# Sums of Mish activations made in SBUF for eleven of the twelve quads, with the order of issue made anew

## The chip, the cores and the metric

The kernel runs on one core of one Trainium2 chip. The metric is device time of one execution in microseconds (us); lower is better. Five engines each run their own list of instructions in order: TensorE (PE in the profile), VectorE (DVE), ScalarE (ACT), GpSimd (POOL) and SyncE (SP), which issues most of the DMAs. [...]

## The reference

Two blocks read the same activations `x` (2048 tokens, 640 features, float32), and a sigmoid gate mixes their results.

```python
x = A_x
g = _sigmoid((x * gate_w).sum(-1, keepdims=True))
a = _A_ref(x, A_wqkv, A_wo)          # 32 heads of 20, window of 8 positions, dilation 2
b = _B_ref(x, B_w1, B_b1, B_w2)      # 640 -> 1728, Mish, -> 640
return g * a + (1 - g) * b
```

```python
h = jnp.einsum("bsd,df->bsf", x, w1) + b1
sp = jnp.log1p(jnp.exp(-jnp.abs(h))) + jnp.where(h > 0, h, jnp.zeros_like(h))
act = h * jnp.tanh(sp)
return jnp.einsum("bsf,fd->bsd", act, w2)
```

## The kernel before

**Products.** Every float32 operand of TensorE is split into a high part (ScalarE, L458) and a low part (VectorE or GpSimd, L461), and each product is made of three matmuls (L517 to L519). Many products are arranged in the manner of Strassen and Winograd: blocks of two row groups by two column groups are made with seven products in place of eight, from sums of operands made beforehand.

**Quads.** The first product of block B (`x` by `w1`) is done in twelve quads. `quad(q, P, R)` makes the four blocks of hidden rows `q` and `q + 7` for the token blocks `2P` and `2P + 1`; q runs from 0 to 5 and P over 0 and 1, and a quad's number is q + 7P, so 0 to 5 and 7 to 12. A quad has eight groups of matmuls on TensorE, 54 matmuls in all, in the PSUM banks `one`, `five`, `two_`, `three` and `four`; there are seven banks for all users. Between the groups stand ScalarE copies from bank to bank (L1061). Two results end in the banks `one` and `two_`; the other two need a further addition on VectorE (`closed`, L1011 or L1094), which leaves them in the SBUF tiles `z12` and `z5`. Mish is applied to all four.

**What the second product needs.** The second product (`w2`) again works with sums of the four activations 11, 12, 21, 22 of a quad: t1 = 11 - 12, t3 = 22 - 12, t2 = 22 + t1 and t4 = t2 - 21 (12 and 21 are stored with their sign turned). All seven, 11, 21, 22 and t1 to t4, go to blocks in DRAM (`act...` and `actt...` in the profile), since they are read much later.

**The two ways to make the sums.** In `mish` (L860) every activation is put into the DRAM blocks, the first addend by plain DMA on SyncE's queue (`put`, L853), the further ones by accumulating DMAs issued by GpSimd (`plus`, L856, issue at L857); of the four `plus` of a quad two take their addend from DRAM. An activation's SBUF tile is free as soon as these transfers have read it. In `added` (L1000) the four activations stay in SBUF: m11 and m12 in the two buffers of the ring `hb`, the others in `z12` and `z5` of the ring `z` (four buffers). L1006 and L1008 are its Mish and sign change. The raw 11, 21 and 22 are put to DRAM; then `total` (L1015), on VectorE or GpSimd, adds in place: t1 into m11, t3 into m12, t2 into z5, t4 into z12, and each is put to DRAM. An addition in place waits until the put of the value that it overwrites has landed; t2 waits for t1 and t3, t4 for t2. Both ways have seven puts for a quad. The set `ADDED` names the quads of the second kind: before, quad 11 alone.

**Order.** The program is recorded as some 2,750 tasks, and a table `ISSUE` gives by their numbers the order for each engine, written out in full; `TAKEN` gives for each buffer ring which engine's task takes the next buffer. `Plan.run` walks through these lists, assigns buffers and banks by its own estimates (`LAG`, `ADDING`, the `size` of a DMA), and makes GpSimd's additions wait for the start of certain VectorE instructions (`follow`). The estimates don't reach the chip; the order, the buffers and the waits do. Loads and stores share SyncE's one list, `plus` and GpSimd's arithmetic share GpSimd's. Between the quads stand the q, k, v products of attention (`qkv`, two to a head group, 15 matmuls each); VectorE works through the attention (L570 to L617) all the while. `mlp1_rest` (L1101) makes the last 64 hidden rows in a flat tile of the ring `pair` (23 places).

Of the kernel before, what the change touches and what calls it, by code (L numbers as in the profile page):

```python
# [25 lines left out]
ROW = 2 * QF  # L26
# [12 lines left out]
ADDED = set([11])  # L39
# [27 lines left out]
class Task:  # L67
# [8 lines left out]
    "PE": """1 96-110 115 120 125 130 145 135 140 232 290 240 236 244 267 298 294 263 302 376 377 380 381 386 388 425 389 390 426 429 430  # L76
435 464 437-439 487 488 491 492 456 497 499 468 460 500 501 536 544 540 548 619 620 623 624 629 631 632 650 651 633 654 655
660 662 663 681 664 739 740 685 693 743 744 689 749 751-753 770 774 778 782 914 909 893 944 919 929 924 945 948 949 954 956
957 1066 1067 958 1070 1071 1076 1078 1107 1079 1080 1102 1097 1112 1175 1176 1179 1180 1185 1187 1206 1188 1189 1246 1210
1218 1247 1250 1251 1214 1256 1289 1301 1297 1293 1258-1260 1357 1358 1403 1361 1362 1364 1366-1368 1404 1407 1408 1413 1415  # L80
1440 1416 1417 1443 1442 1441 1457 1458 1480 1479 1460 1459 1481 1493 1494 1530 1529 1508 1495 1482 1507 1509 1531 1496 1532
1510 1555 1556 1558 1628 1557 1627 1629 1778 1630 1779-1789 1799 1800 1825 1826 1836 1837 1871-1882 1924-1935 1945 1946 1958
1959 1969 1970 1996-2007 2035-2042 2049 2050 2060 2061 2071 2072 2088-2095 2137-2144 2163 2164 2174 2175 2185 2186 2205-2212
2235-2246 2256 2257 2269 2270 2280 2281 2300-2311 2344-2355 2365 2366 2376 2377 2387 2388 2404-2415 2441-2448 2455 2456
2468-2478 2572 2479 2573 2577 2578 2593 2582 2584 2587 2594 2598 2590 2599 2603 2605 2627 2608 2704 2631 2611 2729 2705 2730
2734 2709 2735 2710 2726 2714 2739 2741 2716 2744 2719 2747 2722 2751""",
    "ACT": """7 4 10 13 16 19 25 31 22 47 28 44 41 35 38 116 56 121 72 50 117 59 126 118 62 111 122 53 119 131 127 128 76 123 136 124 146
137 90 132 147 112 141 78 113 142 160 94 88 114 129 74 148 143 233 291 149 163 234 133 212 134 209 144 241 138 242 228 139
92 184 154 237 166 226 224 230 187 238 243 239 292 245 246 169 299 235 190 293 295 268 264 269 286 252 303-305 300 296 378
# [97 lines left out]
class Plan:  # L187
# [3 lines left out]
    ADDING = 5400  # L191
# [133 lines left out]
def kernel(ctx: ExitStack, tc: tile.TileContext, x, wq, wo, w1, b1, w2, out):  # L325
# [1427 lines left out]
```

## Time and profile before

| | us |
|---|---|
| median of 3 runs | 620.06 (619.36, 620.06 and one of 3496.55) |
| the profiled execution | 620.14 |
| its span | 618.4 |
| DVE busy | 563.1 |
| ACT busy | 390.1 |
| mean granted TensorE clock | 0.996 |

The span reaches from the first to the last instruction that the profiler saw. The 2,669 matmuls are pipelined: a row of the timeline gives 0.39 us for one of 512 columns, but the next starts 0.23 us later, so starts are what is compared. PE busy is the share of the time in which at least one runs. A busy engine need not be the bound; a wait on TensorE is.

By line, the page has 26, 13 and 11 issues of accumulating DMAs at L857 from DRAM blocks, from `hb` and from `z`, and 2 more from `pair`: 52.

### The profile page before, as it was taken

How to read it: one execution, taken by the hardware profiler on the slowest of the kernel's cores; microseconds unless marked ns; L12 is line 12 of the kernel's file. 1: busy time of each engine (PE TensorE's matmuls, PEld its weight loads, DVE VectorE, ACT ScalarE, POOL GpSimd, SP SyncE). 2: the span in 40 equal slices, each digit the busy share in tenths (PEclk: the TensorE clock that was granted, in tenths of full speed). 3: DMA queues.
4: the chain of work that ended last, by engine and by line, in shares of the span. 5: the costliest groups of instructions: out<-in, count | busy, mean ns of one | idle time of the engine just before them, and what ended most of it. 6: DMA issues, size and time to landing. Idle time of an engine off the chain costs nothing.

```text
span 618.4 us, 8933 instructions
## 1 busy us (share of the span) xinstructions
PE 608.9 (98%) x2669; PEld 501.1 (81%) x2669; DVE 563.1 (91%) x519; ACT 390.1 (63%) x878; POOL 348.3 (56%) x327
## 2 busy tenths in 40 slices
PE   9999999999999999899999999999999999999997
PEld 6888888877887888688888888887778888888886
DVE  5489999999998999879999999999999999998872
ACT  6564765667757667683478778476777563495640
POOL 2444655545365863575468658968756594614330
PEclk9999999999999999899999999999999999999999
DMA  9636499799999999999999999999999999996733
GB/s 320 215 108 197 121 260 300 194 284 252 296 236 290 234 258 281 276 242 298 279 305 270 330 303 295 271 300 299 326 355 323 302 346 317 331 363 215 244 104 137
DMA packets 109298, 165.03 MB, mean 267 GB/s; under 512 B 12464, under 2 KB 51120, under 8 KB 109216
## 3 DMA queue, kind: packets, MB, share of 16 engines
q1 hardware_dynamic: 102144, 151.60, 75.1%
q0 software_dynamic: 7104, 12.85, 13.7%
q8 instruction: 21, 0.34, 0.2%
q14 instruction: 29, 0.24, 0.1%
HBM read 95.45 MB, written 66.40 MB: 262 GB/s over the span
## 4 chain that ended last, share of the span: by engine, by line
PE 78%; DMA 7%; DVE 4%; ACT 4%; issue 3%; POOL 2%; SPq 2%; ACTq 0%; POOLq 0%; DVEq 0%
PE bank L517 25%; PE bank L519 25%; PE bank L518 25%; POOL pair L461 2%; SPq L467 2%; DMA raw<-in_w 1%; DMA pair<-actt 1%; DVE pr L570 1%; ACT pair L458 1%; DMA raw<-in_x 1%; PE bank L659 1%; DMA hb<-in_w 1%; DVE pair L461 1%; DMA raw<-in_wq 1%; DMA act<-pair 1%
## 5 line engine op out<-in xcount | busy, mean ns | idle before, releaser
L518 PE MATMUL bank<-pair,pair 128*128 128x512 f32 (+2 forms) x742 | 288.1, 388 | 0.4 <-POOL pair L461 0.3
L517 PE MATMUL bank<-pair,pair 128*128 128x512 f32 (+2 forms) x742 | 287.9, 388 | 0.7 <-ACT hx L669 0.7
L519 PE MATMUL bank<-pair,pair 128*128 128x512 f32 (+2 forms) x742 | 287.5, 387 | 0.0
L461 POOL TENSOR_TENSOR pair<-raw,pair 128x512 fp32r<-128x512 f32 (+3 forms) x84 | 106.4, 1274 | 103.5 <-ACT pair L458 35.8
L517 PEld LDWEIGHTS bank<-pair,pair 128*128 128x128 f32 x742 | 139.5, 188 | 29.5 <-ACT hx L669 1.1
L518 PEld LDWEIGHTS bank<-pair,pair 128*128 128x128 f32 x742 | 139.5, 188 | 29.3 <-POOL pair L461 1.3
L519 PEld LDWEIGHTS bank<-pair,pair 128*128 128x128 f32 x742 | 139.5, 188 | 28.0 <-POOL pair L461 0.4
L461 POOL TENSOR_TENSOR pair<-pair 128x512 fp32r<-128x512 f32 (+2 forms) x78 | 97.8, 1273 | 37.5 <-DVE pair L461 8.8
L458 ACT ACTIVATE pair<-pair 128x512 fp32r<-128x512 f32 (+2 forms) x147 | 83.2, 609 | 40.2 <-DMA pair<-actt 17.7
L570 DVE TENSOR_TENSOR pr<-kvq,side 128x2560 f32<-128x2560 f32 x32 | 90.1, 2815 | 4.3 <-ACT side L576 3.4
L617 DVE TENSOR_REDUCE kvq<-pr 128x320 f32<-128x2560 f32 x32 | 90.1, 2816 | 0.8
L608 DVE TENSOR_TENSOR pr<-kvq,side 128x2560 f32<-128x2560 f32 x32 | 90.2, 2818 | 0.7
L573 DVE TENSOR_REDUCE lg<-pr 128x128 f32<-128x2560 f32 x32 | 90.0, 2812 | 0.4
L458 ACT ACTIVATE pair<-raw 128x512 fp32r<-128x512 f32 (+4 forms) x123 | 73.2, 616 | 22.4 <-POOL raw L914 7.3
L665 ACT ACTIVATE kvq<-bank 128x320 f32<-128x320 f32 x64 | 27.5, 433 | 43.0 <-PE bank L519 42.9
L914 POOL TENSOR_TENSOR raw<-raw,raw 128x256 f32<-128x256 f32 (+2 forms) x34 | 35.1, 1033 | 25.2 <-DVE pair L461 13.1
L461 DVE TENSOR_TENSOR pair<-pair 128x512 fp32r<-128x512 f32 (+2 forms) x69 | 45.7, 697 | 0.6 <-ACT pair L458 0.4
L517 PE MATMUL bank<-kvq,pair 128*128 128x512 f32 x102 | 40.7, 399 | 3.0 <-ACT bank L1061 3.0
L519 PE MATMUL bank<-kvq,pair 128*128 128x512 f32 x102 | 40.5, 397 | 0.0
L518 PE MATMUL bank<-kvq,pair 128*128 128x512 f32 x102 | 40.3, 395 | 0.0
L1061 ACT ACTIVATE bank<-bank 128x512 f32<-128x512 f32 x36 | 20.9, 582 | 28.7 <-PE bank L519 24.0
L461 DVE TENSOR_TENSOR pair<-raw,pair 128x512 fp32r<-128x512 f32 (+4 forms) x39 | 28.1, 734 | 9.1 <-ACT pair L458 9.1
(138 smaller groups left out, 643.6 us busy)
## 6 DMA issues: line engine op xcount, KB each, us to landing
pair<-actt SPq DMA_DIRECT2D x54, 256.0 KB, 4.5
pair<-act SPq DMA_DIRECT2D x38, 256.0 KB, 4.4
raw<-in_wq SPq DMA_DIRECT2D x36, 248.0 KB, 5.2
raw<-in_w SPq DMA_DIRECT2D x34, 256.0 KB, 3.4
raw<-in_x SPq DMA_DIRECT2D x29, 256.0 KB, 5.4
actt<-hb SPq DMA_DIRECT2D x28, 256.0 KB, 5.4
actt<-z SPq DMA_DIRECT2D x24, 256.0 KB, 4.9
act<-z SPq DMA_DIRECT2D x24, 256.0 KB, 4.3
```

The lines of the kernel that those rows point to most:

```text
L458: a = add("ACT", act_ns(n), lambda: A.activation(hi(), raw(), AF.Copy), after, rank=rank, take=take, hold=hold, kind="hi")
L461: return (V if e == "DVE" else G).tensor_tensor(lo(), raw(), hi().bitcast(F32), op=OP.subtract)
L517: nc.tensor.matmul(ps, ah, bh, start=first, stop=False, skip_group_check=more)
L518: nc.tensor.matmul(ps, ah, bl, start=False, stop=False, skip_group_check=more)
L519: nc.tensor.matmul(ps, al, bh, start=False, stop=last, skip_group_check=more)
L570: return V.tensor_tensor(pr, window(kv, s0, 0), qs[:, :, None, :].to_broadcast([128, 2, W, QF]), op=OP.mult)
L573: return V.tensor_reduce(lg_w[:, s0:s0 + 2], pr.rearrange("p s w (h d) -> p s w h d", d=DH), op=OP.add, axis=AX.X)
L608: return V.tensor_tensor(twos, vw, pw[:, :, :, :, None, None].to_broadcast([128, 2, W, HQ, DH // 2, 2]), op=OP.mult)
L617: return step("DVE", 2740, lambda: V.tensor_reduce(q[:, s0:s0 + 2].rearrange("p s (f j) -> p f s j", j=2), by_place, op=OP.add, axis=AX.X) ...
L665: a = add("ACT", 330, lambda: A.activation(kv[:, 7 + s], ps.t[:, QF:3 * QF].rearrange("p (a b) -> p a b", a=2), AF.Copy), [done] + before, ...
L914: return (V if e == "DVE" else G).tensor_tensor(t.t[:, i:i + n], a.t[:, j:j + n], b.t[:, k:k + n], op=op)
L1061: return add("ACT", 590, lambda: A.activation(to.t, of.t, AF.Copy), after, rank=-0.6, take=[to], hold=[of], kind=kind)
```

## The change

`ADDED` now holds the numbers 0 to 11. Number 6 is no quad and 11 was in it, so ten more quads (0 to 5 and 7 to 10) go through `added`; quad 12 still goes through `mish`. That takes out 40 of the 52 accumulating DMAs and puts 40 additions at L1015 in: in all 44 of them, 36 on GpSimd (4 before) and 8 on VectorE (none before). The number of puts on SyncE's queue is the same, and so is all work of TensorE. Where an addition or a low part may go to VectorE or GpSimd, the new table has some of them changed over; VectorE has 524 rows for 518. ScalarE has 876 rows for 880: activation tables are loaded 21 times for 25, going by the rows at L595, L869 and L1006.

The five tables of `ISSUE` and the strings of `TAKEN` are new throughout. On TensorE the new order differs from the old by changes of place over a few tasks; from task 1778 on it is the same. Estimates of the plan are new as well (`LAG` of SP, `ADDING`, the sizes of five kinds of DMA), which act on the chip only through buffers, banks and waits.

```diff
@@ -36,7 +36,7 @@
-ADDED = set([11])
+ADDED = set([0,1,2,3,4,5,6,7,8,9,10,11])
@@ -73,122 +73,122 @@
 ISSUE = {
-    "PE": """1 96-110 115 120 125 130 145 135 140 232 290 240 236 244 267 298 294 263 302 376 377 380 381 386 388 425 389 390 426 429 430
...
+    "PE": """1 96-110 115 120 125 135 145 130 140 244 232 290 240 236 294 302 263 267 298 376 377 380 381 383 385 425 386 387 426 429 430
...
-    LAG = {"PE": 220, "ACT": 220, "DVE": 200, "POOL": 150, "SP": 2850}
-    ADDING = 5400
+    LAG = {"PE": 220, "ACT": 220, "DVE": 200, "POOL": 150, "SP": 2550}
+    ADDING = 3100
...
-                    after, rank=1.0, hold=hold, size=81920, late=late) for g in range(4)]
+                    after, rank=1.0, hold=hold, size=110592 if late == 0 else 44000, late=late) for g in range(4)]
...
-                            w, rank=-1.0, size=(b - a) * (hi - lo) * ROW * 4) for a, b in ((0, 112), (112, 127))]
+                            w, rank=-1.0, size=(b - a) * (hi - lo) * ROW * (6 if a == 0 else 15)) for a, b in ((0, 112), (112, 127))]
...
-        return dma(lambda: blk[key][rows], src, after, rank=0.5, hold=hold, size=(rows.stop - rows.start) * 2048)
+        return dma(lambda: blk[key][rows], src, after, rank=0.5, hold=hold, size=262144 if rows.stop - rows.start > 64 else 209715)
...
-        d = dma(tall, lambda: h_d[tb], d, hold=[b], size=131072)
+        d = dma(tall, lambda: h_d[tb], d, hold=[b], size=209715)
```

In the quoted list of TensorE, 376 to 390 are the parts of quad 0 (before 376, 377, 380, 381, 386, 388, 389, 390; now 376, 377, 380, 381, 383, 385, 386, 387) and 425 and what follows those of quad 1: the two quads follow one another with no other product between them, before and now.

The two functions of quads that the prediction speaks of are `added`, whose core is this (the same before and after):

```python
        m11, m12 = h_buf(), h_buf()
        a11 = active(q, lambda: one.t, m11, [p2], False, [m11], [one])
        s11 = stored("11", m11, a11)
        a12 = active(q, lambda: two_.t, m12, [p4], True, [m12], [two_])
        ...
        t1 = total(m11, m12, s11 + [a12])
        ...
        t3 = total(m12, z5, [a22, t1])
        t2 = total(z5, m11, s22 + [t1, t3])
        t4 = total(z12, z5, s21 + [t2])
```

and `plus`, which it replaces. Two places show what moved. The first is GpSimd's list in the first half of the quads with P = 1, before. `actt_P_kc_n` and `act_P_kc_n` are DRAM blocks of the activations, `hb` and `z` the SBUF tiles of a quad's activations, `pair` the split operands of TensorE, `raw` tiles that loads arrive in.

```order
L857 DMA actt_1_0_148<-actt_1_0_134 128x512
L857 DMA actt_1_1_135<-hb_2477 128x512
L857 DMA actt_1_0_162<-z_2303 128x512
L461 TENSOR_TENSOR pair_2509<-raw_2193,pair_2509 128x512
L461 TENSOR_TENSOR pair_2506<-raw_2402,pair_2506 128x512
L461 TENSOR_TENSOR pair_2546<-raw_2422,pair_2546 128x496
L461 TENSOR_TENSOR pair_2563<-raw_2431,pair_2563 128x496
L857 DMA actt_1_1_149<-actt_1_1_135 128x512
L461 TENSOR_TENSOR pair_2582<-raw_2535,pair_2582 128x512
L461 TENSOR_TENSOR pair_2569<-raw_2321,pair_2569 128x496
```

Now GpSimd's list has there, for quads 7 and 8:

```order
L1015 TENSOR_TENSOR hb_2252<-hb_2252,hb_2312 128x512
L461 TENSOR_TENSOR pair_2298<-raw_2056,pair_2298 128x512
L1015 TENSOR_TENSOR hb_2312<-hb_2312,z_2225 128x512
L1015 TENSOR_TENSOR z_2225<-z_2225,hb_2252 128x512
L1015 TENSOR_TENSOR z_2314<-z_2314,z_2225 128x512
L461 TENSOR_TENSOR pair_2358<-raw_2267,pair_2358 128x496
L461 TENSOR_TENSOR pair_2377<-raw_2271,pair_2377 128x512
L1015 TENSOR_TENSOR hb_2481<-hb_2481,z_2416 128x512
L461 TENSOR_TENSOR pair_2363<-raw_2175,pair_2363 128x512
L461 TENSOR_TENSOR pair_2511<-raw_2425,pair_2511 128x512
L1015 TENSOR_TENSOR z_2416<-z_2416,hb_2392 128x512
```

The issues of accumulating DMAs are gone, and additions stand between the low parts in their place; a low part now stands behind an addition that may wait for a put.

The second place is ScalarE's list ahead of the first copy of quad 9 from bank to bank, which TensorE's next group waits for. Before:

```order
L458 ACTIVATE pair_2546<-raw_2422 128x496
L872 ACTIVATE z_2453<-z_2453 128x512
L665 ACTIVATE kvq_220<-bank_66 128x320
L458 ACTIVATE pair_2563<-raw_2431 128x496
L667 ACTIVATE kvq_220<-bank_66 128x160
L458 ACTIVATE pair_2569<-raw_2321 128x496
L1061 ACTIVATE bank_68<-bank_63 128x512
```

Now, with the same copy (the source is `bank_63` again) in the third row, and the second copy of the quad in the tenth:

```order
L458 ACTIVATE pair_2553<-raw_2478 128x496
L458 ACTIVATE pair_2558<-raw_2470 128x496
L1061 ACTIVATE bank_69<-bank_63 128x512
L665 ACTIVATE kvq_220<-bank_67 128x320
L667 ACTIVATE kvq_220<-bank_67 128x160
L458 ACTIVATE pair_2571<-raw_2447 128x496
L458 ACTIVATE pair_2581<-raw_2514 128x512
L458 ACTIVATE pair_2584<-raw_2474 128x496
L665 ACTIVATE kvq_220<-bank_65 128x320
L1061 ACTIVATE bank_66<-bank_69 128x512
L458 ACTIVATE pair_2598<-raw_2365 128x512
```

Before, `pair_2546` takes the place that the flat tile of `mlp1_rest` for token block 0 (`pair_2249`) had held, 15 rows behind that tile's last ScalarE instruction; now the tile that follows this flat tile in its place is `pair_2598`, 27 rows behind it and behind both copies.

More of the change, by code (lines that the diff above doesn't have):

```diff
@@ L80 @@
[L80 to L83, printed above, removed]
@@ new lines @@
+2468-2479 2572 2573 2577 2578 2593 2582 2584 2587 2590 2594 2598 2599 2603 2605 2627 2729 2704 2608 2631 2611 2730 2705 2709
+2734 2710 2735 2714 2726 2739 2716 2741 2719 2744 2722 2747 2751""",
+    "ACT": """7 4 19 10 13 16 41 25 47 22 44 31 35 28 38 116 117 59 118 111 72 62 112 56 50 121 126 119 76 53 136 131 122 132 123 74 113
[10 rows of a table added]
+1098-1101 1009 1003 1177 1103 1104 1012 1018 1006 1113 1181 1027 1105 1114 1106 1110 1187 1021 1183 1127 1178 1030 1015 823
+1192 1115 1193 1024 1189 1190 1130 1207 1198 1248 1249 1116 1211 1133 1252 1111 1212 1121 1036 1213 1215 1216 1136 1208 1045
@@ new lines @@
+1209 1151 1290 1219-1221 1258 1217 1033 1254 1291 1238 1302 1154 1294 1235 1303 1244 1292 1241 1260 1263 1264 1261 1359 1269
+1295 1363 1296 1435 1298 1449 1474 1157 1360 1299 1365 1369 1309 1455 1491 1405 1406 1300 1371 1374 1372 1412 1438 1375 1380
+1312 1414 1059 1304 1160 1452 1395 1423 1524 1424 1477 1444 1409 1418 1428 1445 1315 1461 1447 1462 1333 1464-1466 1488 1446
[13 rows of a table added]
+2654 2731 2687 2685 2713 2738 2715 2750 2727 2740 2752""",
+    "DVE": """0 8 5 14 11 20 17 42 26 23 32 48 45 29 39 36 63 69 70 51 71 57 73 77 84-86 216 218 75 161 162 164 165 185 93 213 186 167 168
@@ new lines @@
+188 189 155 170 171 191 192 172-177 283 178 179 311 392 312 398 194-197 396 198 199 314 315 441 375 200 447 201 317 450 413
+318 202 335 412 424 336 203 503 338 339 320-322 509 323 341 342 324-326 478 327 328 557 558 635 560 641 344 329 420 561
+345-347 644 348 708 666 563 718 349 702 350 564 351 672 352 566 353 567 568 581 679 582 569-572 755 584 761 585 573 574 587
+766 588 575 855 861-863 590 591 791 878 792 899 592 875 882 593 934 594 595 794 795 902 596-598 983 960 797 966 599 986 815
+816 798 818 819 800 1082 801 1088 802-804 989 1086 805-808 1095 821 1013 1019 822 809 1128 1191 1129 1197 824-826 1131 827
@@ new lines @@
+1200 1132 828 1134 829 830 1135 831 832 1137 1138 833 1122 1152 1153 1139-1141 1053 1142 1262 1155 1268 1156 1143-1145 1373
+1158 1310 1159 1146 1379 1311 1313 1422 1314 1161 1162 1427 1163 1164 1478 1165-1168 1316 1169 1170 1317 1334 1335 1319 1320
+1538 1550 1321 1322 1535 1534 1323 1539 1536 1324 1325 1540 1541 1537 1337 1338 1326 1327 1340 1328 1849 1564 1750 1341 1740
+1565 1343-1345 1815 1727 1346 1567 1568 1347 1829 1348 1349 1840 1350-1352 1570 1938 1571 1859 1893 1588 1902 1949 1589 1573
@@ new lines @@
+1591 1592 1574-1576 1954 1577-1580 1976 1915 1594 1581 1595 1979 1648 1649 2025 2031 2028 2056 1597 1582 1598 2045 2053 1599
[3 rows of a table added]
+1666 1681 1682 2459 2375 2403 1683 2428 1684 2383 1685-1688 2400 1689 2158 2440 2424 2434 2514 2505 2467 2451 2464 2526 2454
+1690 2499 2489 2502 2558 2547 2523 2517 2511 2495 2520 2693 2560 2541 2634 2532 2579 2562 2538 2544 2564 2571 2553 2566 2568
+2588 2575 2556 2576 2616 2703 2596 2600 2585 2646 2694 2625 2700 2591 2597 2650 2665 2648 2622 2660 2662 2669 2666 2670 2674
@@ new lines @@
+2676 2606 2609 2671 2612 2680 2655 2672 2668 2684 2711 2732 2707 2658 2736 2686 2717 2733 2708 2742 2745 2723 2748 2720""",
+    "POOL": """68 60 2 54 79 95 89 229 91 87 219 274 276 210 220 278 225 231 287 253 227 256 277 271 360 262 362 289 285 363 259 250 364
+401 369 371 403 373 409 405 411 445 452 475 418 454 476 477 520 422 522-524 531 507 529 512 514 516 533 535 480 699 609 612
[9 rows of a table added]
+2619 2561 2550 2696 2702 2644 2667 2664 2678 2652 2690 2682 2692 2688 2701 2698""",
+    "SP": """6 3 9 18 12 15 24 40 46 21 43 30 27 34 64 65 55 37 61 58 66 49 67 33 52 80 82 81 150 214 151 211 215 153 222 273 152 208 83
[24 rows of a table added]
@@ L173 @@
+2689 2691 2712 2737 2718 2610 2613 2697 2607 2728 2743 2746 2724 2749 2721 2592 2753""",
 }
 TAKEN = {
-    "bank": ("0000000000000000000000010101011010010100100000101101011001000101000000001000011010110000010110010001010000010011011"
-        "01001011100100111111100000011110010000111001011101111101001011111"),
-    "raw": ("4444444444444444444444442444434444444344444344444424444444424444444444444444444444444444444444444444444444444444444"
-        "44444444444444414144444444444444444444444443444444344424444214441444444444"),
@@ L179 @@
-    "pair": ("1111111111111111111111111111111111111111111111111111111111111111111111111111111112111111111111111111111241111441411"
-        "1414444414141411411444414414141422141414144414414444444444444444444444444444444444444444444444444444444444444444444"
-        "44444414441444144444414444414444414444414444444144444444441144111111"),
+    "bank": ("0000000000000000000000010110011101000101000000101100110100101001000000000100011010101000010110000110000010001101011"
+        "01001011100010111101110000011110100000111001011101110010111011111"),
@@ new lines @@
+    "raw": ("4444444444444444444444442444434444444443444344444434444444344444444444444444444444444444444444444444444444444444444"
+        "44444444444444441444144444444444444444444443444444434244442444141444444444"),
+    "pair": ("1111111111111111111111111111111111111111111111111111111111111111111111111111211111111111111111111111111241111441114"
+        "4141444441441111411444414414142214411414444144141444444444444444444444444444444444444444444444444444444444444444444"
+        "44444141444144444444414444441444414144444444441444444444441141411111"),
```

35 lines of the change are left out of this document (8 added, 27 removed), and 124 rows, old and new, of the table ISSUE.

## The prediction

> **What bounds the kernel now.** I read the page first. Its first part gives the share of the span for which each engine is busy.
>
> ```profile
> span 618.4 us, 8933 instructions
> ...
> PE 608.9 (98%) x2669; PEld 501.1 (81%) x2669; DVE 563.1 (91%) x519; ACT 390.1 (63%) x878; POOL 348.3 (56%) x327
> ```
>
> TensorE works through 98% of the span, so no change beside it can win much: 618.4 - 608.9 = 9.5 us is all the time in which no matmul runs, start and end included. The question is where TensorE waits, and whether the change adds waits. The busy time by stretches of 15.5 us answers the first; the columns are the stretch, its length, then busy time and number of instructions of PE, PEld, DVE, ACT and POOL, then the granted clock, the DMA share and GB/s.
>
> ```profile
> 124.00:139.50 15.50, 14.86 (x67) 12.06 (x66) 14.76 (x8) 10.55 (x32) 7.65 (x8) 1.00 1.02 281
> 139.50:155.00 15.50, 15.22 (x68) 12.28 (x67) 15.02 (x13) 11.04 (x21) 8.83 (x10) 1.00 0.91 255
> 155.00:170.50 15.50, 15.50 (x71) 13.08 (x70) 15.33 (x17) 11.12 (x21) 5.45 (x7) 1.00 1.03 296
> ...
> 186.00:201.50 15.50, 14.82 (x67) 12.16 (x66) 13.28 (x18) 11.27 (x31) 8.60 (x10) 1.00 1.07 288
> ...
> 248.00:263.50 15.50, 13.43 (x53) 10.68 (x52) 13.46 (x11) 10.28 (x31) 8.18 (x8) 0.89 0.99 278
> ```
>
> Most stretches read like 155.00:170.50: PE 15.50 of 15.50. In the part with the quads (62 to 330 us) four fall short, by 0.64, 0.28, 0.68 and 2.07 us; the one from 248.00 stands out, also by its clock of 0.89. TensorE's timeline shows why.
>
> ```profile
> 255.93 0.39 PE L519 MATMUL bank<-kvq,pair 128*128 128x512 f32 x1
> 258.39 0.79 PE L517 MATMUL bank<-kvq,pair 128*128 128x512 f32 x1 [2.07 <-ACT bank L1061]
> ...
> 262.10 0.39 PE L517 MATMUL bank<-pair,pair 128*128 128x512 f32 x1
> ...
> 263.92 0.39 PE L519 MATMUL bank<-kvq,pair 128*128 128x512 f32 x1
> ```
>
> From 262.10 to 263.92 eight matmuls start in 1.82 us, one every 0.227 us. From 255.93 to 262.10 there are ten, which at that pace take 2.27 us and took 6.17: this place costs 3.9 us, of which 2.07 are the wait and the rest matmuls at about half pace behind it. [...]
>
> TensorE waited for a copy from bank to bank on ScalarE (L1061). ScalarE's timeline has that copy late because of an instruction ahead of it.
>
> ```profile
> 252.27 0.26 ACT L671 ACTIVATE zt<-bank 128x1 f32<-128x1 f32 x2
> 255.18 0.62 ACT L458 ACTIVATE pair<-raw 128x496 fp32r<-128x496 f32 x1 [2.66 <-issue]
> ...
> 257.74 0.59 ACT L1061 ACTIVATE bank<-bank 128x512 f32<-128x512 f32 x1
> ```
>
> The split at 255.18 had waited 2.66 us. It writes the tile `pair_2546`, in the place of the flat tile of `mlp1_rest`, which two puts were still reading. The DMAs of 236 to 258 us, with their time from issue to landing in the last column:
>
> ```profile
> q0 software_dynamic: 576, 1.04, 27.0%
> ...
> actt<-actt POOLq DMA_DIRECT2D x1, 256.0 KB, 9.4
> actt<-hb POOLq DMA_DIRECT2D x1, 256.0 KB, 8.9
> actt<-z POOLq DMA_DIRECT2D x1, 256.0 KB, 10.4
> ...
> act<-pair SPq DMA_DIRECT2D x1, 128.0 KB, 8.3
> ```
>
> The put `act<-pair` took 8.3 us to land. SyncE's timeline has its issue:
>
> ```profile
> 246.74 0.57 SPq L467 DMA_DIRECT2D act<-pair  x1
> ```
>
> So it landed at 246.74 + 8.3 = 255.04, just ahead of the split. Three accumulating DMAs were under way, which took 8.9 to 10.4 us, and their queue held 27% of the DMA engines. Two of the other three waits follow from DMAs too, a load of `wq` and one of `x`:
>
> ```profile
> 132.54 1.13 ACT L458 ACTIVATE pair<-raw 128x496 fp32r<-128x496 f32 x2 [1.41 <-DMA raw<-in_wq]
> ...
> 189.58 0.63 ACT L458 ACTIVATE pair<-raw 128x512 fp32r<-128x512 f32 x1 [1.75 <-DMA raw<-in_x]
> ```
>
> So TensorE's waits among the quads come mostly from late DMAs, passed on by ScalarE's fixed order.
>
> **The change part by part.** *Accumulating DMAs, 40 of 52 removed.* The page gives the queues:
>
> ```profile
> q1 hardware_dynamic: 102144, 151.60, 75.1%
> q0 software_dynamic: 7104, 12.85, 13.7%
> ```
>
> Forty of 256 KB are 10.5 of the 12.85 MB of q0, so by bytes 11.2 of the 13.7% go: 0.112 x 618.4 = 69 us of all 16 engines. They lie among and just behind the quads, where the stretches above have a DMA share of 0.91 to 1.07; of the 268 us from 62 to 330 it is about a quarter. None of this is on TensorE's path in itself. What it is worth is the waits:
> - the place at 255.93: -3.9 us. At a landing of 4.3 us, what an undisturbed put takes (row below), the split could start by about 251. Beside that the new order puts this tile's successor behind both copies of the quad. Two independent reasons, so I take all of it; ends -3.9 and 0.
> - the other three: 0.64 + 0.28 + 0.68 = 1.6 us; ends -1.6 and 0. Two came from loads, and every operation of theirs has moved, so I take half, -0.8.
>
> *Issues of those DMAs on GpSimd removed, additions put in.*
>
> ```profile
> L857 POOL DMA_DIRECT2D actt<-actt x26 | 22.9, 901 | 10.9 <-DMA actt<-z 9.6 <-DMA o<-ot 1.3
> ```
>
> 40 x 0.9 = 36 us leave GpSimd. 32 additions of 1.30 us (row at L1015 below) come, 41.6 us: +5.6 us on an engine with 348.3 of 618.4 busy. Its cover is its own idle time; I take 0. VectorE gets 8 x 0.68 = 5.5 us (0.684 for an operation of this size, last fence). It is at 15.33 of 15.50 in the stretch from 155.00, and the attention that it works on is needed by the output projection; but matmuls of the second product, which wait for activations and not for attention, stand between. With 524 rows for 518 it also hands some over. I take 0, ends 0 and +5.5.
>
> *ScalarE's four table loads less, and the puts.* The four loads are on no path by themselves, since ScalarE is at 390.1; 0. Puts are as many as before; three of them in each quad now wait for an addition, and stand in SyncE's list at the place where the plan expects it. A put that comes late holds up the loads behind it: this is part of the next term.
>
> *Tiles held longer.* This is the new wait. The two `hb` tiles of a quad were free when the puts of Mish had read them. Now m11 is held until t2 has been made of it. Bank `one` stays full until m11's buffer is free for the next quad. The one quad done so before gives the hold:
>
> ```profile
> L1006 ACT ACTIVATE hb<-bank,bias x2: 659/674/690, 318.7 to 322.0; 128x512 f32<-128x512 f32 x2
> ```
> ```profile
> L1015 POOL TENSOR_TENSOR z<-z,hb x1: 1302/1302/1302, 341.3 to 341.3; 128x512 f32<-128x512 f32 x1
> ```
>
> From the Mish into m11 at 318.7 to the end of t2 at 341.3 + 1.3 = 342.6 it is 23.9 us, in a place where nothing pressed. The shortest is the chain itself: 27 matmuls (6.1 us) until the last bank is done, 0.68 for `closed` (a VectorE operation of this size), 0.67 for Mish, a put's landing and the addition of 1.30.
>
> ```profile
> act<-z SPq DMA_DIRECT2D x24, 256.0 KB, 4.3
> ```
>
> That is 6.1 + 0.7 + 0.7 + 4.3 + 1.3 = 13.1 us. Two quads that follow one another directly reach the same point 54 x 0.227 = 12.25 us apart, and TensorE has another 6.1 us of the quad's own matmuls before it wants banks for the next: 18.35 us are covered. So at 13.1 nothing is lost, and at 23.9 there is a wait of 5.5 us. In TensorE's list four pairs follow directly (0 and 1, 3 and 4, 7 and 8, 11 and 12); elsewhere products of attention, 15 matmuls or 3.4 us each, stand between. I take the middle of the hold, 18.5, which is 0.15 over the cover, and for order on GpSimd and SyncE going wrong once a wait like the one at 186.00, 0.68: 4 x 0.15 + 0.7 = +1.3 us. Ends: 0, and 4 x 5.5 = 22 with 1.6 of half pace for each, 28.
>
> The sum, against the profiled execution's own 620.14 (span 618.4 and 1.74 around it; the median of the runs is 620.06): 620.14 - 3.9 - 0.8 + 1.3 = 616.7 us.
>
> **The rivals.**
> 1. *All waits among the quads go.* For it: the DMA engines get a quarter of their time back where they were full. Then 3.9 + 1.6 go and nothing comes: 614.6, and less where smaller ones elsewhere go too. Against it: each of the small ones had a chain of several engines.
> 2. *Nothing is gained.* The change takes out a transfer that was mostly hidden, and waits of the same size stand elsewhere, since all operations have moved: 620 to 621. For it: three of the four waits were under 0.7 us, which any order has.
> 3. *The tiles are the bound.* Slower than before. Two of the four tight pairs at the hold of 23.9 cost 2 x (5.5 + 1.6) = 14.2 us: 620.14 - 4.7 + 14.2 = 629.6. It decides from a hold of 18.35 us; three such pairs pass 2%. For it: the only quad seen held m11 for 23.9. Against it: that quad's additions stood behind other work on GpSimd, since nothing waited for them.
> 4. *VectorE becomes the bound.* It is busy for 13.3 to 15.3 of 15.5 us in the stretches above, so what it gets more may come out at the end: 616.7 + 5.5 = 622.2. Its own operations can be held up by GpSimd's beside it:
>
> ```profile
> L461 DVE TENSOR_TENSOR pair<-raw,pair x39: 282/684/1526, 4.9 to 597.9; 128x512 fp32r<-128x512 f32 x27, 128x496 fp32r<-128x496 f32 x6, 128x498 fp32r<-128x498 f32 x4, 128x128 fp32r<-128x128 f32 x1
> ```
>
> A subtraction of 0.684 us has taken up to 1.526, 0.84 more. If this happened at each of 32 more additions on GpSimd, VectorE had 27 us more, and its idle time of 618.4 - 563.1 = 55 us lies mostly at the start and the end: up to 616.7 + 5.5 + 27 = 649. Against it: the median is 0.684, so it is rare, and the additions are tied to long VectorE operations that read one input from PSUM. [...]
>
> **How the numbers follow.** My forecast (615 to 618.5) gets 0.43; rival 1 (611.5 to 615) 0.16; rival 2 (618.5 to 621.5) 0.16; rival 4 at its small price (621.5 to 625) 0.09; rival 3 up to two pairs (625 to 632.5) 0.10; more pairs, or VectorE at its high price, 0.05; under 611.5 0.01. The predicted time is that of the likeliest, 616.7. The range 612 to 628 leaves out some 0.14; it takes in the ends of the terms for the waits and for VectorE, and of rival 3 what one pair costs (620.14 - 4.7 + 7.1 = 622.5), not two. The bound of 2% (12.4 us, about what a measurement of this kernel can tell from no change) is at 607.7 and 632.5: faster 0.01, as only 9.5 us are idle at all; slower 0.05; within 0.94.
>
> **What would show it.** Right: no wait of TensorE over 1 us among the quads and a granted clock of 1.00 in every stretch from 62 to 310; q0 at about 2.5%; the DMA share there nearer 0.75; 36 additions of 1.30 on GpSimd and 8 of 0.68 on VectorE. Wrong: waits of TensorE for Mish (L1006) or for a copy behind it, which is rival 3; `hb` or `z` as what ScalarE waits for; VectorE's attention ending more than 5 us later (rival 4); or TensorE's waits as long as before in other places (rival 2).

## The result, and the profile after

| | before | changed |
|---|---|---|
| median of 19 runs, us | 619.36 (616.12 to 623.17, and one of 3496.55) | 616.07 (614.29 to 617.59) |
| ratio, 95% interval | 1 | 0.9945 (0.9926 to 0.9965) |
| span of the profiled execution, us | 618.4 | 615.2 |

The changed kernel is 3.3 us faster, a difference that the interval holds to be real, though small. Its runs also lie closer together: 3.3 us from lowest to highest, against 7.1 (without the one execution of 3496.55 us, which lies far from all the others). The first part of the page of the changed kernel (share of the span for which each engine is busy):

```profile
span 615.2 us, 8925 instructions
...
PE 606.5 (99%) x2669; PEld 499.9 (81%) x2669; DVE 567.3 (92%) x523; ACT 387.6 (63%) x874; POOL 363.4 (59%) x323
```

TensorE's busy time fell by 2.4 us, the time without any matmul from 9.5 to 8.7, which together is the 3.2 us of the span. The matmuls are the same; some 1.8 of the 2.4 us are the matmuls at half pace behind the wait at 255.93, which now keep the full pace. The rest is not half pace: behind the wait at 134.80 to 135.83 us, for one, the next start comes after 0.34 us and those behind it after 0.23 again. A row of 0.39 us covers the first part of each wait, so busy time holds some of the small waits too. Where the time without matmuls lies is seen in four long stretches (columns as in the prediction: stretch, its length, then busy time and number of instructions of PE, PEld, DVE, ACT, POOL, granted clock, DMA share, GB/s). The kernel before:

```profile
62.00:200.00 138.00, 136.40 (x606) 113.35 (x605) 131.88 (x104) 91.86 (x203) 75.86 (x76) 1.00 0.90 247
200.00:330.00 130.00, 127.90 (x557) 105.18 (x556) 122.04 (x92) 85.43 (x198) 78.75 (x73) 0.99 0.97 271
330.00:470.00 140.00, 139.10 (x613) 114.02 (x611) 136.57 (x116) 101.69 (x231) 102.99 (x98) 1.00 1.01 308
470.00:560.00 90.00, 90.00 (x398) 74.44 (x397) 87.22 (x100) 54.46 (x112) 49.77 (x44) 1.00 1.00 334
```

The changed kernel:

```profile
62.00:200.00 138.00, 138.00 (x618) 115.68 (x617) 134.42 (x109) 96.80 (x214) 90.15 (x80) 1.00 0.70 217
200.00:330.00 130.00, 129.95 (x576) 107.74 (x575) 127.40 (x98) 88.33 (x202) 86.26 (x72) 1.00 0.80 247
330.00:470.00 140.00, 138.74 (x616) 115.17 (x616) 137.41 (x117) 96.38 (x229) 103.07 (x98) 1.00 0.99 300
470.00:560.00 90.00, 88.15 (x383) 71.42 (x382) 85.98 (x103) 54.54 (x108) 43.60 (x36) 1.00 0.96 317
```

Among the quads (the first two rows) TensorE stood idle for 1.60 + 2.10 = 3.70 us and now for 0.05. The DMA share fell from 0.90 and 0.97 to 0.70 and 0.80. VectorE was busy for 2.5 and 5.4 us more in the same stretches, of which its eight additions are 5.5. Behind the quads it is the other way round. TensorE's idle time went from 0.90 to 1.26 and from 0 to 1.85, and in the first 15.5 us, not shown in these rows, from 1.21 to 1.93. So 3.65 us of idleness were won and 2.93 lost in these two executions. The losses differ between executions: in other runs below with the same order up to 470 us, TensorE is idle for 0 to 2.4 us from 330 to 470, and the start comes either way. The short stretches that answer to those in the prediction, with the stretch at 418 and the two at the end in which the new waits lie:

```profile
124.00:139.50 15.50, 15.50 (x71) 12.98 (x70) 15.31 (x8) 10.89 (x28) 12.83 (x11) 1.00 0.80 244
139.50:155.00 15.50, 15.50 (x70) 12.90 (x70) 15.09 (x17) 8.37 (x19) 8.66 (x9) 1.00 0.76 251
...
186.00:201.50 15.50, 15.50 (x71) 13.04 (x70) 15.33 (x15) 10.04 (x30) 10.62 (x9) 1.00 0.64 194
...
248.00:263.50 15.50, 15.50 (x70) 12.84 (x69) 14.74 (x13) 10.79 (x27) 9.65 (x8) 1.00 0.72 209
...
418.50:434.00 15.50, 14.70 (x65) 11.84 (x64) 15.29 (x13) 9.48 (x21) 12.52 (x13) 1.00 1.00 312
...
527.00:542.50 15.50, 14.96 (x64) 11.49 (x62) 12.32 (x13) 6.03 (x12) 6.25 (x6) 1.00 1.02 318
542.50:558.00 15.50, 14.19 (x60) 11.08 (x60) 15.05 (x21) 13.72 (x27) 6.85 (x4) 1.00 0.98 350
```

The page's queues and puts, with the share of 16 engines, and the median time from issue to landing:

```profile
q1 hardware_dynamic: 102144, 151.60, 77.4%
q0 software_dynamic: 1344, 2.36, 2.5%
...
actt<-hb SPq DMA_DIRECT2D x28, 256.0 KB, 2.6
act<-z SPq DMA_DIRECT2D x24, 256.0 KB, 3.0
actt<-z SPq DMA_DIRECT2D x24, 256.0 KB, 3.5
```

The accumulating queue is down from 13.7% to 2.5%, and these puts of 256 KB land in 2.6, 3.0 and 3.5 us, where they took 5.4, 4.3 and 4.9.

### The profile page after: what moved, and what is told of

Read it like the earlier page. It is cut to its first block, busy times and chain, and to the rows that moved or that the text cites. A ratio compares the mean times of both kernels' runs of the same rounds, so it can differ in the third digit from the quotient of the medians.

```text
span 615.2 us, 8925 instructions
## 1 busy us (share of the span) xinstructions
PE 606.5 (99%) x2669; PEld 499.9 (81%) x2669; DVE 567.3 (92%) x523; ACT 387.6 (63%) x874; POOL 363.4 (59%) x323
## 4 chain that ended last, share of the span: by engine, by line
PE 78%; DVE 10%; DMA 7%; issue 2%; ACT 1%; SPq 1%; POOL 1%; DVEq 0%; POOLq 0%; ACTq 0%
PE bank L518 26%; PE bank L519 26%; PE bank L517 26%; DMA pair<-actt 3%; DVE kvq L617 2%; DVE pr L608 2%; DVE pair L461 2%; DVE lg L573 1%; DVE pr L570 1%; DMA raw<-o 1%; DMA pair<-s 1%; DMA pair<-wt 1%; DMA hb<-in_wq 1%; SPq L467 1%; DMA h<-pair 1%
## 5 line engine op out<-in xcount | busy, mean ns | idle before, releaser
L461 POOL TENSOR_TENSOR pair<-raw,pair 128x512 fp32r<-128x512 f32 (+3 forms) x85 | 108.5, 1289 | 49.7 <-ACT pair L458 14.0
L461 POOL TENSOR_TENSOR pair<-pair 128x512 fp32r<-128x512 f32 (+2 forms) x78 | 98.5, 1278 | 49.0 <-ACT pair L458 12.2
L458 ACT ACTIVATE pair<-pair 128x512 fp32r<-128x512 f32 (+3 forms) x147 | 84.8, 610 | 48.9 <-DMA pair<-act 21.5
L570 DVE TENSOR_TENSOR pr<-kvq,side 128x2560 f32<-128x2560 f32 x32 | 90.0, 2812 | 5.4 <-ACT side L576 4.8
L617 DVE TENSOR_REDUCE kvq<-pr 128x320 f32<-128x2560 f32 x32 | 90.1, 2815 | 0.6
L458 ACT ACTIVATE pair<-raw 128x512 fp32r<-128x512 f32 (+3 forms) x123 | 73.4, 618 | 22.7 <-PE bank L519 5.3
L461 DVE TENSOR_TENSOR pair<-pair 128x512 fp32r<-128x512 f32 (+3 forms) x69 | 49.0, 735 | 3.9 <-ACT pair L458 3.7
L518 PE MATMUL bank<-kvq,pair 128*128 128x512 f32 x102 | 39.9, 391 | 0.6 <-DVE kvq L461 0.6
L519 PE MATMUL bank<-kvq,pair 128*128 128x512 f32 x102 | 39.9, 391 | 0.0
L517 PE MATMUL bank<-kvq,pair 128*128 128x512 f32 x102 | 39.9, 391 | 0.0
L461 DVE TENSOR_TENSOR pair<-raw,pair 128x512 fp32r<-128x512 f32 (+3 forms) x38 | 28.6, 767 | 3.8 <-ACT pair L458 3.7
```

The source lines that it names most:

```text
L458: a = add("ACT", act_ns(n), lambda: A.activation(hi(), raw(), AF.Copy), after, rank=rank, take=take, hold=hold, kind="hi")
L461: return (V if e == "DVE" else G).tensor_tensor(lo(), raw(), hi().bitcast(F32), op=OP.subtract)
L517: nc.tensor.matmul(ps, ah, bh, start=first, stop=False, skip_group_check=more)
L518: nc.tensor.matmul(ps, ah, bl, start=False, stop=False, skip_group_check=more)
L519: nc.tensor.matmul(ps, al, bh, start=False, stop=last, skip_group_check=more)
L570: return V.tensor_tensor(pr, window(kv, s0, 0), qs[:, :, None, :].to_broadcast([128, 2, W, QF]), op=OP.mult)
```

## The experiments

The kernel before was timed again beside each group of runs, with medians from 619.17 to 619.69 us; ratios are against it.

### The transfers alone, in the old order

```diff
-lambda: G.dma_start(out=blk[key][:rows], in_=src(), accum_op=OP.add, ...)
+lambda m=1 if key[1] * 7 + key[2] in (0, 1, 2, 3, 4, 5, 7, 8, 9, 10) else rows: G.dma_start(out=blk[key][:m], in_=src()[:m], accum_op=OP.add, ...)
```

> The kernel before, every instruction of every engine at its place, but the 40 accumulating DMAs of the ten quads move one row (2 KB) in place of 256 KB; so all rows but one of those sums are left out. It tells what the transfers alone cost. Theory (the transfers delayed other DMAs, and the order is secondary): the put from the flat tile that took 8.3 us lands in about 4.3, the split behind it no longer waits 2.7 us, TensorE does not wait at 256 us, and of the other waits among the quads about half goes: 3.9 + 0.8 of 619.4, 614.5 to 616.5 us. Rival (the order, in which the split stands ahead of the copy, made the wait): the wait at 256 stays above 1.5 us and the time at 618.5 to 620.

614.97 us, ratio 0.9926 (0.9899 to 0.9953). This is the whole gain, and perhaps more, with no addition in SBUF and no row moved; its interval overlaps that of the changed kernel, so the two can't be told apart. Shrinking the transfers also shortened GpSimd's own waits ahead of their issues, from 31.2 to 26.7 us in all, and the time that the source tiles are held; the run does not separate this from the load on the DMA engines. The place at 256 us shows the predicted chain link by link. The put from the flat tile landed in 2.6 us (8.3 before), the split ran without a wait, and then the copy that TensorE waits for and VectorE's low parts. First the issue of the put on SyncE's queue, then ScalarE, then VectorE:

```profile
244.36 0.46 SPq L467 DMA_DIRECT2D act<-pair  x1
```
```profile
250.32 0.66 ACT L458 ACTIVATE pair<-raw 128x496 fp32r<-128x496 f32 x1
...
253.09 0.60 ACT L1061 ACTIVATE bank<-bank 128x512 f32<-128x512 f32 x1
```
```profile
255.83 1.27 DVE L461 TENSOR_TENSOR pair<-raw,pair 128x496 fp32r<-128x496 f32 x2
```

### The order alone, at that one place

ScalarE's list, one row moved:

```diff
+L1061 ACTIVATE bank_68<-bank_63 128x512
 L458 ACTIVATE pair_2546<-raw_2422 128x496
...
 L458 ACTIVATE pair_2569<-raw_2321 128x496
-L1061 ACTIVATE bank_68<-bank_63 128x512
```

> The kernel before with one row of ScalarE's list moved: the first bank copy of quad 9 (L1061) stands ahead of the split that waited 2.7 us, in place of six rows behind it. All accumulating DMAs stay. Theory (that one place costs TensorE 3.9 us, and the order alone can avoid it): the split still waits until the put has landed at about 255, TensorE does not wait at 256, 615.5 to 616.5 us. Rival (the wait only moves on, to the second copy of the quad or to the rows between): TensorE waits over 1 us between 256 and 270, 618 to 620 us.

620.55 us, ratio 1.0012 (0.9981 to 1.0043): nothing gained. In its profile TensorE does not wait at 256 us any more, but 1.14 us at 259, for the second copy of the quad; with the slower first matmul behind it that place costs 1.4 us in place of 3.9. The 2.5 us were lost again later:

```profile
200.00:330.00 130.00, 128.30 (x565) 105.45 (x564) 123.51 (x93) 86.28 (x199) 80.48 (x75) 1.00 0.97 276
330.00:470.00 140.00, 138.40 (x604) 112.18 (x604) 134.58 (x115) 100.97 (x232) 101.29 (x96) 1.00 0.99 303
470.00:560.00 90.00, 88.54 (x387) 71.96 (x386) 86.05 (x97) 53.58 (x109) 48.23 (x43) 1.00 0.99 325
```

Against the kernel before TensorE works 0.7 and 1.46 us less from 330 to 560. That nothing was gained is what the twelve runs show; where it was lost is less sure, since the profiled execution, of 622.31 us, is 1.8 above their median, and the run with small transfers has TensorE idle for 2.11 us from 330 to 470 as well. The late split had a second victim. VectorE makes the low parts of the same tiles, and its row behind the long reduction had waited for ScalarE before (first fence, the kernel before) and still did (second, this run):

```profile
259.98 1.28 DVE L461 TENSOR_TENSOR pair<-raw,pair 128x496 fp32r<-128x496 f32 x2 [2.01 <-ACT pair L458]
```
```profile
259.54 1.28 DVE L461 TENSOR_TENSOR pair<-raw,pair 128x496 fp32r<-128x496 f32 x2 [1.81 <-ACT pair L458]
```

With the small transfers this wait is gone. The last reduction of attention on VectorE (L617) tells how VectorE as a whole stands; the kernel before, this run, the small transfers, and the changed kernel:

```profile
539.24 2.80 DVE L617 TENSOR_REDUCE kvq<-pr 128x320 f32<-128x2560 f32 x1
```
```profile
541.79 2.81 DVE L617 TENSOR_REDUCE kvq<-pr 128x320 f32<-128x2560 f32 x1
```
```profile
534.19 2.81 DVE L617 TENSOR_REDUCE kvq<-pr 128x320 f32<-128x2560 f32 x1
```
```profile
533.44 2.81 DVE L617 TENSOR_REDUCE kvq<-pr 128x320 f32<-128x2560 f32 x1
```

The two kernels that gained have VectorE 5 to 6 us earlier; the one in which only TensorE was spared has it no earlier. These are single executions, so the size is rough. From the start of this reduction to the end of the span it is 79.2, 78.7 and 79.1 us in the three kernels with the old end, and 81.8 in the changed kernel: of the 5.8 us that its VectorE is ahead there, 2.6 are given back at the end.

### VectorE, more and less

```diff
-return step("DVE", 2740, lambda: V.tensor_reduce(...), kind="qk sum")
+return step("DVE", 2740, lambda: [V.tensor_reduce(...) for i in range(2 if u % 2 and s0 == 0 else 1)][-1], kind="qk sum")
```

> The changed kernel with four of the 32 long reductions of attention (L617, 2.82 us each) done twice, spread over the attention; nothing else is changed and the output is the same. VectorE has 11.3 us more. Theory (VectorE's attention sets the end beside TensorE, so a wait won on TensorE alone is lost again later): the last L617 begins 6 to 11 us later than 533.4, and the time is 621 to 627. Rival (TensorE alone sets the end, VectorE has slack): 616 to 618.

622.21 us, ratio 1.0054 (1.0029 to 1.0079): 6.1 us more than the changed kernel for 11.3 us of work. The last reductions end at 542.66 us, 6.4 later than 536.25:

```profile
536.99 5.67 DVE L617 TENSOR_REDUCE kvq<-pr 128x320 f32<-128x2560 f32 x2
```

So about 5 of 11 us found idle time, and the rest came out at the end nearly one to one. The opposite run moved the eight additions of VectorE to GpSimd's list:

> The changed kernel with the eight additions that stand on VectorE moved to GpSimd, each at the place in GpSimd's list where the plan has that time; VectorE has 8 x 0.68 = 5.5 us less, GpSimd 8 x 1.30 = 10.4 more. Theory (VectorE sets the end beside TensorE): the last L617 begins 2 to 5 us earlier than 533.4 and the time is 613 to 615.5. Rival (no slack is won, or the longer hold of the tiles takes it back): 615.8 to 618.

615.96 us, ratio 0.9945 (0.9924 to 0.9965), the same as the changed kernel, and the last L617 began at 534.4 us, not earlier. VectorE's busy time fell by 3.1 us and not by 5.5 (564.2 for 567.3), so its other operations took longer, and it did not finish sooner. The theory holds in one direction only: lateness of VectorE reaches the end in part, and neither a wait less on TensorE alone (the moved copy) nor less work on VectorE alone brought a gain. That both engines are too near their bound for one to win anything by itself is the likeliest reading; no run shows it directly.

### The tiles held longer

```diff
-        def total(to, other, after):
+        long = q + KH * P in (0, 3, 7, 11)
+        def total(to, other, after, n=0):
             def run(e):
+                for i in range(n):
+                    (V if e == "DVE" else G).tensor_tensor(to.t, to.t, other.t, op=OP.add)
                 return (V if e == "DVE" else G).tensor_tensor(to.t, to.t, other.t, op=OP.add)
...
-        t2 = total(z5, m11, s22 + [t1, t3])
+        t2 = total(z5, m11, s22 + [t1, t3], 6 * long)
```

> The changed kernel with the third addition (t2) of the quads 0, 3, 7 and 11, those with the next quad directly behind them, done seven times in place of once (so that sum has t1 added seven times). m11 is held 6 x 1.30 = 7.8 us longer there: about 21.4 us from its Mish where 13.6 was seen at the quads 3 and 7. Theory (18.35 us of hold are covered): the next quad's first Mish is late by about 3 us at the pairs 3 and 4 and 7 and 8, and TensorE waits 2 to 4 us at two or three of the four pairs, 4 to 10 us more in all: 620 to 626. Rival (the cover is longer, or the next quad finds another buffer): no wait of TensorE by it, under 617.

646.81 us, ratio 1.0443 (1.0386 to 1.0501): 30.7 us more, over three times what was expected. TensorE waits once at each of the four pairs. In this kernel L1005 is the Mish (L1006 elsewhere) and L1014 holds the added additions:

```profile
101.26 0.79 PE L519 MATMUL bank<-kvq,pair 128*128 128x512 f32 x1 [4.81 <-POOL pair L461]
...
168.09 0.80 PE L517 MATMUL bank<-pair,pair 128*128 128x512 f32 x1 [5.80 <-ACT pair L458]
...
260.29 0.80 PE L517 MATMUL bank<-pair,pair 128*128 128x512 f32 x1 [4.59 <-ACT bank L1061]
...
363.12 0.78 PE L518 MATMUL bank<-pair,pair 128*128 128x496 f32 x1 [5.15 <-POOL pair L461]
```
```profile
L1014 POOL TENSOR_TENSOR z<-z,hb 128x512 f32<-128x512 f32 x24 | 32.0, 1334 | 4.4 <-DMA act<-z 1.7 <-DVE hb L1015 1.1
L1005 ACT ACTIVATE hb<-bank,bias 128x512 f32<-128x512 f32 x22 | 15.1, 687 | 39.0 <-POOL z L1015 27.1 <-PE bank L519 10.2 <-POOL pair L461 1.3
```

At three of the pairs ScalarE stood still at the Mish in this row, for 27.1 us in all, until t2 was done; at the pair 11 and 12, whose second quad has its Mish at L869, for another 7.06. What TensorE waits for is not the bank that the Mish would free. It is a split, a low part or a copy that stands behind the Mish in ScalarE's list. Adding 8.2 to 8.6 us of hold (six additions of 1.33, with what lay between) made waits of 4.6 to 5.8 us, so the changed kernel has 2.4 to 3.8 us in hand at these places.

### The transfers put back into the new order

Four runs. The first two add accumulating DMAs to sums of earlier quads:

```diff
+        last = [p for p in sorted(ADDED) if p < q + KH * P][-1:]
+        def total(name, to, other, after):
             def run(e):
+                if last:
+                    G.dma_start(out=blk[name, last[0] // KH, last[0] % KH][:, :], in_=x[0, 0], accum_op=OP.add, ...)
                 return (V if e == "DVE" else G).tensor_tensor(to.t, to.t, other.t, op=OP.add)
```

> The changed kernel, with an accumulating DMA of 256 KB from x to a sum of the quad before issued by GpSimd ahead of each of 40 additions in SBUF (so those sums have x added). The transfers and their issue are back, the new order stays. Theory (the transfers made the waits): waits of TensorE of 0.5 us and more are back among the quads, 618 to 621 us. Rival (the new order made the gain, and the DMA engines have room): no such wait, at most 0.5 us over the changed kernel, 616 to 616.6.

652.93 us, ratio 1.0549 (1.0496 to 1.0602): neither. GpSimd waited ahead of two of the issues, and the additions behind them came late, so ScalarE waited for `hb` (L1005 is the Mish here, L1014 the added issue):

```profile
L1014 POOL DMA_DIRECT2D actt<-in_x x40 | 38.4, 974 | 13.0 <-DMA actt<-z 13.0
...
L1005 ACT ACTIVATE hb<-bank,bias 128x512 f32<-128x512 f32 x22 | 15.1, 685 | 34.5 <-POOL z L1015 18.1 <-DMA actt<-hb 8.4 <-PE bank L519 6.1
```

The experiment had put a wait of its own into GpSimd's list, so it does not measure the transfers. The second run issues behind the addition and to blocks of two quads earlier:

> As the run load_put_back, but each accumulating DMA goes to a sum of two quads earlier, whose put has long landed, and is issued behind the addition, not ahead of it: 36 of them (so those sums have x added). GpSimd never waits for a put that it would not wait for anyway. Theory (the transfers themselves cost about what cutting them in the kernel before gained, 619.6 - 615.0 = 4.6 us; the 33 us more of load_put_back were GpSimd's waits for puts, which held the tiles): 36 of 40 of that and 36 issues of 0.9 us on GpSimd, 619 to 622 us. Rival (the transfers make the waits directly): over 630.

643.43 us, ratio 1.0382 (1.0344 to 1.0421). Its number is that of the rival, but its trace (of the longest of the six executions, 649.63 us) still has GpSimd waiting ahead of an issue (3.75 us at 134.5 us, for a put), so it does not separate them either. The third has plain DMAs to tiles that nobody reads, and no such wait:

```diff
+                G.dma_start(out=dram.tile([128, 512], F32, name=...)[:, :], in_=x[0, 0], ...)
```

> The changed kernel, with a plain DMA of 256 KB from x to a DRAM tile of its own, which nobody reads, issued by GpSimd behind each of the 44 additions in SBUF. It adds as much traffic as the accumulating DMAs had, and the issue of it on GpSimd, but no wait for a put (in load_put_back and load_behind GpSimd waited for puts ahead of some issues). Theory (the traffic costs what small_transfers gained, about 4.6 us, and the rest of the 24 to 33 us of the two other runs was GpSimd's waits): 618 to 623 us. Rival (traffic makes the puts land later, so the additions come later and the tiles are held beyond what ScalarE's order covers): over 630, with ScalarE waiting for hb.

625.58 us, ratio 1.0100 (1.0049 to 1.0152): 9.5 us over the changed kernel, between the two expectations. GpSimd's issues took 0.53 us each and no wait:

```profile
L1013 POOL DMA_DIRECT2D spare<-in_x x44 | 23.1, 527 | 0.0
```

The puts `actt<-hb` landed in 3.7 us (2.6 in the changed kernel) and ScalarE waited 9.4 us for `hb` (4.6 in the changed kernel). Whether the tiles made the difference was asked with four `hb` tiles:

```diff
-SIZES = {"pair": 23, "home": 6, "raw": 9, "hb": 2, "z": 4}
+SIZES = {"pair": 23, "home": 6, "raw": 9, "hb": 4, "z": 4}
```

> The run load_beside (625.6 us) with four hb tiles in place of two, so that a quad's m11 and m12 never wait for the additions of the quad before; all orders are the same. ScalarE waited 9.4 us for hb in load_beside. Theory (beyond the 4 to 5 us that the traffic costs in the old order, the rest of its 9.5 us comes from tiles held longer while the puts land later): no wait of ScalarE for hb, 620 to 622.5 us. Rival (the rest is late loads and late additions on GpSimd, tiles have no part): 624 to 627.

625.11 us, ratio 1.0101 (1.0053 to 1.0148). By the median the rival holds. But the trace in which ScalarE's wait for `hb` is gone is of an execution of 621.12 us, inside the theory's range and 5.4 below the traced one of the run before, and the six reach from 621.05 to 626.25; so what the tiles cost is not settled. That such DMAs, transfer and issue together, are dear in the new order too is shown; why they cost 9.5 us there, where shrinking the transfers gained 4.6 in the old order, stays open. Late loads and 23 us of issues on GpSimd are candidates. The pages show one more: VectorE was busy for 576.2 us in the run with two `hb` tiles and 567.3 in the changed kernel, for the same 523 instructions, and most of that is in a small multiplication of attention, which once took 3.08 us (its median is 0.30). The changed kernel first, then that run:

```profile
L611 DVE TENSOR_TENSOR side<-lg,sm 128x128 f32<-128x128 f32 x32 | 10.2, 318 | 0.4
```
```profile
L611 DVE TENSOR_TENSOR side<-lg,sm 128x128 f32<-128x128 f32 x32 | 17.1, 534 | 0.8 <-ACT side L576 0.4
```

### The old order at the ends

The new waits at the end and the slower start were tried with the old order from there, or up to there, for all engines. At the end:

> The changed kernel up to what the plan begins at 470 us, and from there every engine in the order of the kernel before. Theory (the waits of TensorE from 529 to 551 us, 3.4 us in sum, come from the new order of the end, since the time from the start of the last L617 to the end of the span is 81.8 us and was 79.2): no wait over 0.5 us there, 612.5 to 614.5 us. Rival (TensorE waits there because it is earlier and attention is not): 615.5 to 617.

623.40 us, ratio 1.0071 (1.0046 to 1.0097). TensorE waited 9.70 us at 490 us, at the seam, and not at all from 510 to 558. A later seam:

> As the run old_end, with the seam at 510 us of the plan in place of 470, where SyncE's list is not held up by a store that waits (in old_end TensorE waited 9.9 us at 480 for this). Theory (the 3.4 us of waits from 529 to 551 are the new order's): 612.5 to 614.5 us. Rival (every seam costs more than the waits): over 616.

619.10 us, ratio 0.9999 (0.9970 to 1.0028). TensorE is idle for 2.7 us from 510 to 558, as against 1.85 in the changed kernel. From the start of the last L617 to the end of the span it is 79.1 us with the first seam and 79.9 with the second, near the 79.2 of the kernel before. That agrees with the new order as the cause of the late waits, but does not show it, since everything has time to catch up behind a seam that stalls. At the start:

> The changed kernel with what the plan begins in the first 20 us in the order of the kernel before, on every engine, and everything behind it in the new order. Theory (the 1.4 us that TensorE loses at 4.9 us is the new order's, 0.6 before): 0.8 us less there, 614.5 to 615.8 us. Rival (the start is covered by what VectorE does later, or the seam costs as much): 615.8 to 618.

614.84 us, ratio 0.9913 (0.9881 to 0.9945), the lowest median among those that leave nothing out. Its interval overlaps that of the changed kernel, so a gain over it is likely but not shown. Nor is the start shown to be its cause: TensorE works 14.29 of the first 15.5 us in its profile, but also in that of the run old_end, which begins in the new order. Of the ten profiles that do so, four have 13.3 to 13.6 us there (the changed kernel 13.57) and six 14.2 to 14.3. The new order can lose 0.7 us at the start, then, but does not always.

## Why the prediction was right, and where its steps were off

616.7 was forecast and 616.07 measured. Part of that is errors that cancel.

- **The stall at 255.93, -3.9.** Gone, and by the predicted chain: the run with small transfers has the put landed in 2.6 us and neither wait, in the old order. Of the two independent reasons given, the first is enough. The second, the order, is not: the run that moved the copy alone won some 2.5 us on TensorE and nothing at the end. What failed there is the view on which the whole sum rests, that a wait of TensorE taken away is time won. That the wait counted here because VectorE was relieved by the same cause is the likeliest reading, from the four times of L617 above; no run relieved VectorE alone at this place.
- **The other three waits, half of 1.6.** All went: 15.50 of 15.50 in each of the three stretches. The term was too small by 0.8 us. TensorE's busy time fell by 2.4 us, of which the step above had 1.8; the other 0.6 is in no term.
- **Tiles held longer, +1.3.** Nothing of it came. The hold was taken as 18.5 us, and at the pairs 3 and 4 and 7 and 8 it was 13.6 and 13.7, near the 13.1 of the chain itself. These are the first Mish, the end of t2, and the next quad's Mish, at the quads 3 and 4:

```profile
138.20 0.69 ACT L1006 ACTIVATE hb<-bank,bias 128x512 f32<-128x512 f32 x1
...
151.87 0.69 ACT L1006 ACTIVATE hb<-bank,bias 128x512 f32<-128x512 f32 x1 [3.46 <-POOL z L1015]
```
```profile
150.53 1.31 POOL L1015 TENSOR_TENSOR z<-z,hb 128x512 f32<-128x512 f32 x1 [1.05 <-DVE hb L1015]
```

  ScalarE did wait 3.46 us for t2, and TensorE had that much in hand. But the cover of 18.35 us was reckoned from the banks, and the bound is ScalarE's order: 13.6 + 2.4 and 13.7 + 3.8 make it 16.0 and 17.5 at these two pairs. At the pairs 0 and 1 and 11 and 12 the holds were 16.3 and 15.7, and the cover some 20 and 19. The price beyond it was about right: 5.5 + 1.6 us for a pair at a hold of 23.9, and 7.7 us (30.7 by four) were measured at holds of 21.8 to 25.1. (For the half pace the place at 255.93 itself gives 3.9 - 2.07 = 1.8, not 1.6.) At two of the four pairs rival 3 was closer than it looked.
- **GpSimd and VectorE, 0 each.** Right as far as one run shows it: moving the eight additions to GpSimd, 5.5 us off one engine and 10.4 onto the other, changed nothing. But VectorE has little room; of 11.3 us more, 6.1 came out. The ground of rival 4 is in the traces: in the kernel before all ten low parts of VectorE (L461) of over 0.85 us ran beside an operation of GpSimd (the one at 118.63 us took 1.49, beside GpSimd's from 118.28 to 119.57), while the long multiplications (L570), 30 of 32 beside GpSimd, kept to 2.78 to 2.82. In the changed kernel 18 low parts took over 0.85 us.
- **Waits elsewhere.** Not in the sum at all, only in the list of wrong signs. Start and end lost 2.93 us. The 1.3 us for the tiles that did not come, the 0.8 us more from the small waits and the 0.6 us of busy time are 2.7 us the other way, and so the sum came out. This is luck: none of these terms was foreseen at its size.
- **What would show it.** The clock of 1.00, q0 at 2.5%, 36 additions on GpSimd and 8 on VectorE, and the DMA share (0.70 and 0.80 for 0.75) were as forecast. One sign of being wrong did show: ScalarE waited 4.6 us at the Mish for the addition into `z` (0.8 before), though TensorE waited nowhere for it. The last reduction of attention came 5.8 us earlier, so rival 4 fell; TensorE's waits of 0.2 to 0.6 us from 532 to 551 are a small part of rival 2.

## What to carry to other kernels

When two engines are both over 90% busy, ask of each stall which of them it delays: here a cause that delayed both, slow transfers, was worth its time, and a reorder that spared one of them was worth nothing. A tile's hold is safe not up to the moment its bank is wanted, but up to the moment the waiting instruction delays what stands behind it in its engine's list. To test a transfer's cost, shrink it in place and keep every instruction; adding transfers back brings waits of their own.

## What the runs showed of the hardware

How long TensorE waited does not by itself tell whether its matmuls run at half pace afterwards. Behind a wait of 1.14 us (the moved copy) and one of 1.64 us (the plain DMAs) the next start comes after 0.34 and 0.33 us, and those behind it stay 0.23 us apart. Behind one of 2.08 us in the run with the doubled reductions they are at first 0.23 us apart and then 0.43:

```profile
420.98 0.50 PE L518 MATMUL bank<-pair,pair 128*128 128x512 f32 x1 [2.08 <-POOL pair L461]
...
421.78 0.40 PE L518 MATMUL bank<-pair,pair 128*128 128x512 f32 x1
422.01 0.46 PE L519 MATMUL bank<-pair,pair 128*128 128x512 f32 x1
422.27 0.63 PE L517 MATMUL bank<-pair,pair 128*128 128x512 f32 x1
422.70 0.63 PE L518 MATMUL bank<-pair,pair 128*128 128x512 f32 x1
```

Waits of 1.97 us (the plain DMAs with more tiles) and 2.07 (the kernel before) had the same effect, with starts 0.43 us apart, and so had two waits of 1.37 and 1.05 us with three matmuls between them, in the run with the later seam: there TensorE is idle for 2.4 us from 526.6 to 530.0. In the kernel before the slow starts begin with the first matmul behind the wait (258.39, the next at 258.98), in the run with the doubled reductions 1.3 us behind its end (422.27). But in the first of the runs that put the transfers back (L1009 is `closed` there) a wait of 2.95 us was not followed by them:

```profile
118.67 0.49 PE L517 MATMUL bank<-pair,pair 128*128 128x496 f32 x1 [2.95 <-DVE z L1009]
119.00 0.39 PE L518 MATMUL bank<-pair,pair 128*128 128x496 f32 x1
119.23 0.39 PE L519 MATMUL bank<-pair,pair 128*128 128x496 f32 x1
```

So of the single waits given here, those of 1.14 and 1.64 us brought no half pace, and between 1.97 and 2.95 us both were seen; what decides there, no run shows. The four waits of 4.6 to 5.8 us in the run with the longer hold brought it each time. Behind the one of 4.81 us the next eleven starts took 4.61 us (101.26 to 105.87), where 11 x 0.23 = 2.5 is the full pace. As those places cost 7.7 us each on average, half pace cost an estimated 2 to 3 us at each.
